# Batch 1's second transform stage rewritten from split-precision matmuls on the whole array to radix-two matmuls on its quarters

## The chip, the cores and the metric

The kernel runs on one core of one Trainium2 chip. The metric is the time of one execution on the device, in microseconds; the times given are those of three runs. The profile is one further execution, recorded by the hardware profiler. TensorE is called PE in its rows, VectorE DVE, ScalarE ACT, GpSimd POOL and SyncE SP; PEld is TensorE's weight load.

## What is computed

A long convolution over the sequence by FFT, gated by x, feeds a two-layer MLP with a leaky ReLU:

```python
h_filt = (np.maximum(pos_emb @ w1, 0.0) @ w2) * np.exp(-0.01 * pos)[:, None]
u = x * v                                   # x, v: (2, 12480, 128)
Uf = np.fft.rfft(u, n=2 * S, axis=1)
Hf = np.fft.rfft(h_filt, n=2 * S, axis=0)
y = np.fft.irfft(Uf * Hf[None], n=2 * S, axis=1)[:, :S, :]
a = (x * y).reshape(B * S, D)               # 24960 tokens of 128
h = a @ w_in                                # w_in: 128 x 2048
out = np.maximum(0.01 * h, h) @ w_out       # w_out: 2048 x 128
```

## The kernel before

The transform of a sequence is done in two stages. The first works on 98 rows of tokens and leaves 98 frequencies `k` by 64 positions `m`, real and imaginary, in DRAM (`scr1` for batch 0 and the filter, `scr1b` for batch 1). The second takes a chunk of four `k` (`KC`, so 25 chunks, `NCH`; the last holds two), transforms over the 64 positions (128 rows of real and imaginary parts), multiplies by the filter's spectrum (`hspec`), transforms back and stores to `scr2`. From there the joins (`cin`, `cp`, `cq`) and the fronts (L933 and L952: the last transform, the product with x and a transpose) make the tokens that the MLP eats.

Three stretches follow each other. Up to about 165 us batch 0 and the filter go through the first stage; its loads, and the constants, are issued by SyncE, three chunks ahead. Up to about 331 us comes batch 0's second stage (`fwd`, L136, and `back_halves`, L164). Then the MLP runs to the end over 50 column tiles of up to 512 tokens and 16 blocks of `w_in` each. Every one of these 800 slots has three matmuls of the first layer (`m1`, L1009, into `mh`, a ring of three buffers), an eviction to a high part on ScalarE (`rh`, L1013) and a low part on VectorE (`rl`, L1014), and three matmuls of the second layer (`m2`, L1050 to L1052) for the slot three earlier. Batch 1's whole transform is hidden beside the MLP of batch 0's tokens: the generator `conv1` yields it in pieces, and the loop draws so many pieces a slot as `pace` says, up to the slot `SLOTS`. The order of every engine is thus the order in which the program is written; there is no scheduler.

Batch 1's second stage is `conv1b`. For each chunk: `split` makes a high part `th` (ScalarE) and a low part `tl` (VectorE, both operands in SBUF) of the loaded `bin1`; `three` (L150) does six matmuls with `mb_h` and `mb_l` into the two `cv` banks; ScalarE brings the halves across (`usp`, L551 and L558), VectorE multiplies one product from PSUM (L553), GpSimd the other and adds (`sums`, L517 and L518); then `ph` (ScalarE) and `pl` (GpSimd, L576) split the product, and one chunk later `back` does six matmuls more, which `mixed_evac` (ScalarE, L230) takes to `ct`, one buffer, to be stored by SyncE (L221). The spectrum of a chunk is loaded by two transfers of 64 rows (L498) into `hd`. All of these are single-pass matmuls (fp32r) on 128 rows by 128 columns. Matmuls of plain fp32, as in L136, L164, L933, have two records each in the profile.

Of the kernel before, what the change touches and what calls it, by code (L numbers as in the profile page):

```python
# [8 lines left out]
F32 = mybir.dt.float32  # L9
F32R = mybir.dt.float32r  # L10
# [11 lines left out]
MC1 = 4  # L22
KC = 4
# [7 lines left out]
def tile_conv_mlp(ctx, tc, x, v, pos_emb, w1, w2, w_in, w_out, cf, cr, cg, cb, ci, cw, out):  # L31
# [20 lines left out]
    hspec = dram.tile([NCH, HB, 2, 2, 512], F32, name="hspec")  # L52
# [114 lines left out]
    def even(w):  # L167

        return (w.stop - w.start) // D % 2 == 0

    def back(dp, parts, c):

        for s in range(2):
            for j, w in halves(c):
                m = mixed if even(w) else lambda t: t
                three(dp[s][:, w], (mi_h[j][:, s], mi_l[j][:, s]), (m(parts[0][:, s, w]), m(parts[1][:, s, w])))

    def turned(pool, psum, m2, m1):
# [45 lines left out]
    def mixed_evac(dp, ct, c):

        for s in range(2):
            for _, w in halves(c):
                o, i = ct[:, w.start // D:w.stop // D, s, :], dp[s][:, w]
                if even(w):
                    nc.scalar.copy(o.rearrange("p (h k) d -> p h k d", h=2),  # L230
                                   i.rearrange("p (k d h) -> p h k d", h=2, d=D))
                else:
                    nc.scalar.copy(o, i.rearrange("p (k d) -> p k d", d=D))
            yield
# [8 lines left out]
    with tc.manual_schedule():  # L243
# [22 lines left out]
        with ExitStack() as st:  # L266
# [74 lines left out]
            nc.vector.memset(w1bd, 0.0)  # L341
            for i in range(2):
# [974 lines left out]
```

## Time and profile before

| | us |
|---|---|
| median of three runs | 1618.61 (1617.85 to 1619.16) |
| the profiled execution | 1622.39 |
| its span, first to last instruction | 1620.6 |

| engine | busy us | share of the span |
|---|---|---|
| TensorE | 1559.0 | 96% |
| VectorE | 1129.5 | 70% |
| ScalarE | 995.9 | 61% |
| GpSimd | 748.6 | 46% |

Busy shares are means over stretches with different limits. Batch 1's second stage lies between about 577 and 1013 us. A matmul's duration in the trace includes its run through the array, so that in a row of matmuls each overlaps the next: what one costs is the distance from its start to the next one's start. The same holds for queued instructions on ScalarE.

### The profile page before, as it was taken

What the parts mean: (1) busy time and instruction counts of PE and PEld (TensorE: products, weight loads), DVE (VectorE), ACT (ScalarE), POOL (GpSimd) and SP (SyncE); (2) the same over time, 40 slices, a digit from 0 to 9 for tenths busy, and PEclk for the clock granted to TensorE, in tenths of its full rate; (3) what the DMA queues carried; (4) which work ended last, traced back from release to release, by engine and by line L of the source; (5) the groups of instructions that cost most, each with busy time, mean ns of one, the idle gap of its engine ahead of it and who ended that gap; (6) DMA issues with size and microseconds to landing.
All of it is one profiled execution on the core that took longest, in us unless ns stands there. A gap on an engine that the chain in (4) does not pass through costs nothing.

```text
span 1620.6 us, 27366 instructions
## 1 busy us (share of the span) xinstructions
PE 1559.0 (96%) x9173; PEld 1323.7 (82%) x9173; DVE 1129.5 (70%) x1785; ACT 995.9 (61%) x2108; POOL 748.6 (46%) x804
## 2 busy tenths in 40 slices
PE   6798899899999999999999999999999999999999
PEld 6787555478888888888888888988888888888888
DVE  4676687765777566666677775577777777777777
ACT  2232454435655466777776777677777776777776
POOL 4563121234735257677777775453433533334310
PEclk9899999999999999999999999999999999999999
DMA  8898999966676557666656752321212212122200
GB/s 247 266 297 264 309 318 324 326 177 200 199 200 200 154 155 195 192 181 181 170 164 179 194 141 63 110 95 57 77 58 63 68 63 87 58 63 62 63 11 21
DMA packets 166358, 253.31 MB, mean 156 GB/s; under 512 B 14302, under 2 KB 119026, under 8 KB 163146
## 3 DMA queue, kind: packets, MB, share of 16 engines
q1 hardware_dynamic: 146478, 226.29, 47.2%
q10 hardware_dynamic: 19740, 25.28, 4.6%
q8 instruction: 73, 1.20, 0.3%
q14 instruction: 67, 0.55, 0.1%
HBM read 168.00 MB, written 83.43 MB: 155 GB/s over the span
## 4 chain that ended last, share of the span: by engine, by line
PE 74%; DMA 9%; DVE 6%; ACT 3%; issue 2%; SPq 1%; POOL 1%; ACTq 0%; DVEq 0%; POOLq 0%
PE mh L1009 28%; PE acc L1051 9%; PE acc L1052 9%; PE acc L1050 9%; PE yp L933 4%; PE cv L150 3%; PE cv L454 3%; DMA scr<-ct 3%; PE op L1082 2%; PE zp L952 1%; PE up L136 1%; DMA pos<-in_pos_emb_dram 1%; PE dp L164 1%; DMA scr<-o 1%; PE a L410 1%
## 5 line engine op out<-in xcount | busy, mean ns | idle before, releaser
L1014 DVE SCALAR_TENSOR_TENSOR rl<-mh,rh 128x512 fp32r<-128x512 f32 (+1 forms) x336 | 226.7, 682 | 199.1 <-ACT rh L1013 197.9
L1022 DVE TENSOR_TENSOR rl<-mh,rh 128x512 fp32r<-128x512 f32 (+2 forms) x416 | 277.2, 670 | 83.6 <-ACT rh L1021 75.0
L1017 ACT ACTIVATE mh<-mh 128x512 f32<-128x512 f32 (+2 forms) x416 | 236.3, 568 | 154.0 <-PE mh L1009 113.3
L1009 PE MATMUL mh<-zh,w_in_h 128*128 128x512 f32 (+3 forms) x800 | 316.8, 396 | 3.6 <-DVE rl L1014 2.4
L1009 PE MATMUL mh<-zl,w_in_h 128*128 128x512 f32 (+3 forms) x800 | 300.0, 375 | 0.2 <-POOL zl L966 0.2
L1009 PE MATMUL mh<-zh,w_in_l 128*128 128x512 f32 (+3 forms) x800 | 299.6, 375 | 0.0
L1051 PE MATMUL acc<-rl,w_out_h 128*128 128x512 f32 (+3 forms) x800 | 299.1, 374 | 0.1
L1050 PE MATMUL acc<-rh,w_out_h 128*128 128x512 f32 (+3 forms) x800 | 299.0, 374 | 0.0
L1052 PE MATMUL acc<-rh,w_out_l 128*128 128x512 f32 (+3 forms) x800 | 299.0, 374 | 0.0
L1013 ACT ACTIVATE rh<-mh 128x512 fp32r<-128x512 f32 (+1 forms) x336 | 198.9, 595 | 133.1 <-PE mh L1009 124.3
L966 POOL TENSOR_TENSOR zl<-zf,zh 128x390 fp32r<-128x390 f32 (+24 forms) x110 | 67.8, 630 | 426.5 <-ACT zh L965 403.8
L696 POOL TENSOR_TENSOR cp<-cq,cp 98x256 f32<-98x256 f32 x248 | 194.0, 782 | 32.6 <-DVE cp L684 15.9
L1019 DVE CAST rh<-mh 128x512 fp32r<-128x512 f32 (+2 forms) x208 | 139.3, 670 | 65.9 <-ACT mh L1017 65.5
L1009 PEld LDWEIGHTS mh<-zh,w_in_h 128*128 128x128 f32 x800 | 151.7, 190 | 29.6 <-DVE rl L1014 8.7
L1009 PEld LDWEIGHTS mh<-zh,w_in_l 128*128 128x128 f32 x800 | 151.8, 190 | 19.7
L1051 PEld LDWEIGHTS acc<-rl,w_out_h 128*128 128x128 f32 x800 | 151.2, 189 | 20.2 <-DVE rl L1022 0.4
L1050 PEld LDWEIGHTS acc<-rh,w_out_h 128*128 128x128 f32 x800 | 151.2, 189 | 19.8
L1052 PEld LDWEIGHTS acc<-rh,w_out_l 128*128 128x128 f32 x800 | 151.2, 189 | 19.7
L1009 PEld LDWEIGHTS mh<-zl,w_in_h 128*128 128x128 f32 x800 | 152.2, 190 | 15.6 <-POOL zl L966 0.6
L1021 ACT CAST rh<-mh 128x512 fp32r<-128x512 f32 (+2 forms) x208 | 118.5, 570 | 6.5
L693 POOL TENSOR_TENSOR cq<-cin 98x256 f32<-98x256 f32 x124 | 97.6, 787 | 0.3 <-DMA cin<-scr 0.3
L105 ACT COPY a1s<-a 98x384 f32<-98x384 f32 x64 | 30.7, 480 | 97.3 <-PE a L410 68.7
(170 smaller groups left out, 2529.8 us busy)
## 6 DMA issues: line engine op xcount, KB each, us to landing
cin<-scr SPq DMA_DIRECT2D x318, 98.0 KB
hd<-hspec SPq DMA_DIRECT2D x48, 512.0 KB
bin<-scr SPq DMA_DIRECT2D x23, 768.0 KB
scr<-o SPq DMA_DIRECT2D x28, 588.0 KB
scr<-ct SPq DMA_DIRECT2D x25, 512.0 KB
scr1b<-o SPq DMA_DIRECT2D x32, 392.0 KB
hspec<-hs ACTq DMA_DIRECT2D x48, 256.0 KB
xm<-in_x_dram SPq DMA_DIRECT2D x128, 96.0 KB
```

The source lines that it names most:

```text
L693: eng.tensor_tensor(out=cq[:, p], in0=ci_t[:, 0, :, 0, :], in1=ci_t[:, 0, :, 1, :], op=op)
L696: eng.tensor_tensor(out=cp[:, p, w], in0=cq[:, p], in1=cp[:, p, 1], op=op)
L1009: nc.tensor.matmul(hp, u[:, fs], m, start=(i == 0), stop=(i == 2))
L1013: nc.scalar.activation(out=split2(rh), in_=plain(hp), func=AF.Relu)
L1014: nc.vector.scalar_tensor_tensor(out=split2(rl), in0=plain(hp), scalar=0.0, in1=split2(rh), op0=ALU.max, op1=ALU.subtract)
L1017: nc.scalar.activation(out=hp, in_=hp, func=AF.Lrelu, alpha=0.01)
L1019: nc.vector.tensor_copy(split2(rh), plain(hp))
L1021: nc.scalar.copy(split2(rh), plain(hp))
L1022: nc.vector.tensor_tensor(out=split2(rl), in0=plain(hp), in1=split2(rh), op=ALU.subtract)
L1050: nc.tensor.matmul(ap, w_out_h[:, f, :], rh, start=(f == 0 and not sums(k)), stop=False)
L1051: nc.tensor.matmul(ap, w_out_h[:, f, :], rl, start=False, stop=False)
L1052: nc.tensor.matmul(ap, w_out_l[:, f, :], rh, start=False, stop=(f == NF - 1))
```

## The change

Only batch 1's second stage is done anew. The transform over 64 positions is split in even and odd positions (radix two). The load puts even rows on the upper 64 partitions and odd rows on the lower (two transfers, `scr1b[e::2]`), and `fwd2` does four fp32 matmuls of 64 by 64, one for each half of the rows and of the columns, straight from the loaded tile: no split in high and low parts. `odd` (ScalarE) copies one half's result, VectorE makes sum and difference `u`, multiplies by the imaginary part of the spectrum with a sign for each row (`q`; `sgn`), GpSimd by the real part (`p1`). Four ScalarE copies of 32 rows by 1024 bring `q` to the partner rows (`jq`), late in the chunk's pieces. One chunk later GpSimd adds (`o1`) and makes the sum and difference `pin`, and two chunks later `back2` does four 64 by 64 matmuls; two buffers `ct` are used in turn. The spectrum is stored in another order and loaded by four transfers of 32 rows, the result is stored by two transfers. Constants `mt`, `bt` and `sgn` take the place of `mb_h`, `mb_l`, `mi_h`, `mi_l`. A chunk has 23 pieces instead of 15, and the stage begins after 24 pieces of waiting instead of 12.

```diff
-    hspec = dram.tile([NCH, HB, 2, 2, 512], F32, name="hspec")
+    hspec = dram.tile([NCH, 2, HB, 2, 512], F32, name="hspec")
...
+    mt = const.tile([128, 2, HB], F32, name="mt")
+    sgn = const.tile([128, 1], F32, name="sgn")
+    bt = [const.tile([128, 128], F32, name=f"bt{j}") for j in range(2)]
...
+    def quads(dst, src):
+        for s in range(2):
+            for r in range(2):
+                nc.scalar.copy(dst[HB * s + 32 * r:HB * s + 32 * r + 32, :], src[HB * r:HB * r + 32, s, :])
...
+    def fwd2(up, t, n):
         for s in range(2):
+            for e in range(2):
+                r = slice(HB * e, HB * e + HB)
+                nc.tensor.matmul(up[e][HB * s:HB * s + HB, :n * D].rearrange("p (k d) -> p k d", d=D),
+                                 mt[r, s, :], t[r, :n, s, :], start=True, stop=True)
+    def back2(dp, pin, c):
+        for j, w in halves(c):
+            for s in range(2):
+                r = slice(HB * s, HB * s + HB)
+                for e in range(2):
+                    nc.tensor.matmul(dp[s][HB * e:HB * e + HB, w], bt[j][r, e::2], pin[r, e, w],
+                                     start=True, stop=True)
...
+            for q in range(4):
+                nc.vector.memset(sgn[32 * q:32 * q + 32], -1.0 if q % 2 else 1.0)
...
                     nc.sync.dma_start(out=mb, in_=cb)
+                    for e in range(2):
+                        nc.sync.dma_start(out=mt[HB * e:HB * e + HB].rearrange("p s (r q) -> p (s r) q", r=2),
+                                          in_=cb[e::2].rearrange("p s r q -> p (s r) q")[:, :, :32])
...
-        WAIT = 12
+        WAIT = 24
+        LAST_B = 6
...
             def fetch_h(c):
...
-                for i in range(2):
-                    nc.sync.dma_start(out=h[HB * i:HB * i + HB, :, :, :n * D], in_=hspec[c][:, :, :, :n * D])
+                for s in range(2):
+                    src = hspec[c][s].rearrange("(h q) r w -> q h r w", h=2)
+                    for i in range(2):
+                        q = h[HB * s + 32 * i:HB * s + 32 * i + 32]
...
+                    up = psc["next"]()
+                    fwd2(up, t, n)
+                    yield
...
+                    nc.scalar.copy(odd, up[1][:, :w])
+                    for i, op in enumerate((ALU.add, ALU.subtract)):
+                        nc.vector.tensor_tensor(out=u[:, i, :w], in0=up[0][:, :w], in1=odd, op=op)
+                        yield from rest(2)
+                    for i in range(2):
+                        nc.vector.scalar_tensor_tensor(out=q[:, i, :w], in0=u[:, i, :w], scalar=sgn, in1=h[:, i, 1, :w],
+                                                       op0=ALU.mult, op1=ALU.mult)
+                        nc.gpsimd.tensor_tensor(out=p1[:, i, :w], in0=u[:, i, :w], in1=h[:, i, 0, :w], op=ALU.mult)
+                        yield from rest(2)
+                    fetch_b(c + 3)
+                if 0 < c <= NCH:
...
+                    for i in range(2):
+                        nc.gpsimd.tensor_tensor(out=o1[:, i, :v], in0=o1[:, i, :v], in1=jq[:, i, :v], op=ALU.add)
                         yield
+                if c > NCH:
+                    yield from rest(LAST_B)
+                if c > 1:
+                    dp = psc["next"]()
+                    back2(dp, pin, c - 2)
+                    yield
+                if c > 1:
+                    ct = cts[c % 2]
+                    yield from back_evac(dp, ct, chunk(c - 2)[1])
+                    late = lambda c=c, ct=ct: store_back(1, c - 2, ct, nc.sync)
+                if c < NCH:
+                    jq = held[c] = pool.tile([128, 2, 512], F32, tag="q", name="jq", bufs=2)
+                    for i in range(4):
+                        o = 32 * (i ^ 1)
+                        nc.scalar.copy(jq[32 * i:32 * i + 32, :, :w], q[o:o + 32, :, :w])
                         yield
+                if 0 < c <= NCH:
+                    for i, op in enumerate((ALU.add, ALU.subtract)):
+                        nc.gpsimd.tensor_tensor(out=pin[:, i, :v], in0=o1[:, 0, :v], in1=o1[:, 1, :v], op=op)
+                        yield from rest(2)
...
-        pieces = N1 * (MC1 // 2) * 4 + WAIT + 3 + 15 * NCH - 3
+        pieces = N1 * (MC1 // 2) * 4 + WAIT + 23 * NCH + LAST_B
```

In the orders below the line numbers are those of the kernel that the order is of; in the changed one `m1` is L1012, `m2` L1053 to L1055, `rh` L1016.

TensorE at a forward visit of `conv1b`, before:

```order
L1050 MATMUL acc<-rh,w_out_h 128x512
L1051 MATMUL acc<-rl,w_out_h 128x512
L1052 MATMUL acc<-rh,w_out_l 128x512
L150 MATMUL cv<-th,mb_h 128x512
L150 MATMUL cv<-tl,mb_h 128x512
L150 MATMUL cv<-th,mb_l 128x512
L150 MATMUL cv<-th,mb_h 128x512
L150 MATMUL cv<-tl,mb_h 128x512
L150 MATMUL cv<-th,mb_l 128x512
```

and now:

```order
L1053 MATMUL acc<-rh,w_out_h 128x512
L1054 MATMUL acc<-rl,w_out_h 128x512
L1055 MATMUL acc<-rh,w_out_l 128x512
L172 MATMUL cv<-bin_7764,mt 64x512 x4
L1012 MATMUL mh<-zh,w_in_h 128x512
```

Six matmuls that fill the array have become four that fill a quarter of it each; a back visit (`L181`, `bt`) reads the same.

ScalarE about a chunk's evacuations (`ct`), before:

```order
L507 CAST th<-bin_8943 128x4x128
L1013 ACTIVATE rh<-mh 128x512
L511 CAST th<-bin_8943 128x4x128
L1013 ACTIVATE rh<-mh 128x512 x2
L230 COPY ct_9383<-cv 128x4x128
L1013 ACTIVATE rh<-mh 128x512
L230 COPY ct_9383<-cv 128x4x128
L1013 ACTIVATE rh<-mh 128x512
```

and now, where `pins` is one of the two buffers of `ct`, up to the next chunk's `odd`:

```order
L237 COPY pins<-cv 128x4x128 x2
L1016 ACTIVATE rh<-mh 128x512
L576 COPY jq<-q 32x1024 x2
L1016 ACTIVATE rh<-mh 128x512
L576 COPY jq<-q 32x1024 x2
L1016 ACTIVATE rh<-mh 128x512 x3
L546 COPY odd<-cv 128x512
```

Between two evictions `rh` stood one 512-wide instruction, or none; now two evacuations or two exchange copies stand there in a row.

SyncE in the first stage, about the loads of the constants, before:

```order
L182 DMA ph_305<-in_cf_dram 64x2x50 x2
L361 DMA mb<-in_cb_dram 128x256
L362 DMA mi<-in_ci_dram 128x256
L365 DMA mi_75<-in_ci_dram 64x128 x4
L383 DMA scr_60<-o 98x4x384 x2
```

and now:

```order
L188 DMA ph_307<-in_cf_dram 64x2x50 x2
L361 DMA mb<-in_cb_dram 128x256
L363 DMA mt<-in_cb_dram 64x4x32 x2
L365 DMA mi<-in_ci_dram 128x256
L368 DMA mi_75<-in_ci_dram 64x128 x4
L384 DMA scr_60<-o 98x4x384 x2
```

Two transfers stand ahead of those that were there.

## Rows read from the trace of the kernel before

**Rows 1.** Busy us (instructions) PE, PEld, DVE, ACT, POOL; PEclk, DMA share, GB/s.

```profile
577.00:1013.00 436.00, 430.94 (x2293) 370.70 (x2292) 290.25 (x401) 316.66 (x664) 309.81 (x301) 1.00 0.60 167
```

**Rows 2.** Waits of PE, 577 to 1013 us: total us, times, longest.

```profile
PE mh L1009 <- DVE rl L1014: 2.4, 5, 0.8
```

**Rows 3.** Waits of PEld in the same stretch.

```profile
PEld mh L1009 <- DVE rl L1014: 8.5, 16, 1.2
```

**Rows 4.** Timeline about 651 us: start, length, instruction [idle before it <-releaser].

```profile
651.05 1.08 ACT L230 COPY ct<-cv 128x512 f32<-128x512 f32 x2 [6.19 <-DMA scr<-ct]
651.69 0.48 PE L150 MATMUL cv<-th,mb_h 128*128 128x512 f32 x1 [1.84 <-ACT ct L230]
```

**Rows 5.** Timeline of PE: first of six matmuls of a back visit, and the next.

```profile
695.94 0.38 PE L150 MATMUL cv<-ph,mi_h 128*128 128x512 f32 x1
...
697.23 0.38 PE L1009 MATMUL mh<-zh,w_in_h 128*128 128x512 f32 x1
```

**Rows 6.** Timeline of PE in batch 0's second stage.

```profile
195.70 1.99 PE L164 MATMUL dp<-pin,mi 64*128 64x512 f32 x8
197.52 1.06 PE L846 MATMUL hp<-w,es 64*128 64x128 f32 x16
198.57 1.94 PE L136 MATMUL up<-bin,mb 128*64 128x512 f32 x8
200.31 1.07 PE L799 MATMUL ep<-mb,bin 128*64 128x128 f32 x16
```

**Rows 7.** Timeline of PE about a front.

```profile
627.75 0.38 PE L1052 MATMUL acc<-rh,w_out_l 128*128 128x512 f32 x1
628.06 1.97 PE L933 MATMUL yp<-cp,gt 98*64 98x128 f32 x32
629.96 0.48 PE L1009 MATMUL mh<-zh,w_in_h 128*128 128x512 f32 x1
630.28 0.38 PE L1009 MATMUL mh<-zl,w_in_h 128*128 128x512 f32 x1
```

**Rows 8.** Groups of ACT, 577 to 1013 us: xcount | busy, mean ns | idle before.

```profile
L575 ACT CAST ph<-usp 128x512 fp32r<-128x512 f32 x48 | 29.1, 628 | 0.0
...
L558 ACT COPY usp<-cv 64x512 f32<-64x512 f32 x48 | 27.8, 579 | 1.0
...
L575 ACT CAST ph<-usp 128x256 fp32r<-128x256 f32 x2 | 0.8, 412 | 0.0
```

**Rows 9.** Timeline of ACT while instructions are queued on it.

```profile
693.94 0.61 ACT L507 CAST th<-bin 128x512 fp32r<-128x512 f32 x1
694.45 0.60 ACT L1013 ACTIVATE rh<-mh 128x512 fp32r<-128x512 f32 x1
694.94 0.61 ACT L511 CAST th<-bin 128x512 fp32r<-128x512 f32 x1
```

**Rows 10.** Groups of DVE, 577 to 1013 us.

```profile
L1014 DVE SCALAR_TENSOR_TENSOR rl<-mh,rh 128x512 fp32r<-128x512 f32 x244 | 165.7, 687 | 135.3 <-ACT rh L1013 134.5
L512 DVE TENSOR_TENSOR tl<-bin,th 128x512 fp32r<-128x512 f32 x48 | 57.0, 1201 | 0.6 <-ACT th L507 0.6
L684 DVE TENSOR_TENSOR cp<-cin 98x256 f32<-98x256 f32 x37 | 32.9, 901 | 0.0
L553 DVE TENSOR_TENSOR usp<-cv,hd 128x512 f32<-128x512 f32 x48 | 32.8, 684 | 7.9 <-ACT usp L558 4.9 <-PE cv L150 1.8 <-DMA hd<-hspec 0.9
```

**Rows 11.** Line L684 on DVE, same stretch: duration ns min/median/max.

```profile
L684 DVE TENSOR_TENSOR cp<-cin x37: 407/420/2824, 577.2 to 966.9; 98x256 f32<-98x256 f32 x37
```

**Rows 12.** Groups of POOL, 577 to 1013 us.

```profile
L576 POOL TENSOR_TENSOR pl<-usp,ph 128x512 fp32r<-128x512 f32 x48 | 61.4, 1292 | 50.2 <-ACT ph L575 50.2
```

**Rows 13.** Timeline of SP's issues: start, length from first to last.

```profile
39.52 5.14 SPq L365 DMA_DIRECT2D mi<-in_ci_dram  x4
```

**Rows 14.** Window 40 to 45 us, columns of rows 1.

```profile
40.00:45.00 5.00, 5.00 (x37) 4.98 (x36) 5.00 (x10) 1.63 (x4) 2.68 (x3) 1.00 0.67 159
```

**Rows 15.** Line L498 on SP's queue, 577 to 1013 us: issue ns min/median/max.

```profile
L498 SPq DMA_DIRECT2D hd<-hspec x50: 450/578/1200, 577.4 to 974.1; - x50
```

More of the change, by code (lines that the diff above doesn't have):

```diff
@@ L220, in store_back @@
         k0, n = chunk(c)
+        if b:
+            for e in range(2):
+                eng.dma_start(out=scr2[b][k0:k0 + n].rearrange("k r (m e) d -> e (r m) k d", e=2)[e],
+                              in_=ct[HB * e:HB * e + HB, :n].rearrange("p k s d -> p k (s d)"))
+            return
         eng.dma_start(out=scr2[b][k0:k0 + n].rearrange("k r m e -> (r m) k e"),
                           in_=ct[:, :n].rearrange("p k s d -> p k (s d)"))
[L224 to L234, printed above, removed]
     def back_evac(dp, ct, n):
@@ L490, in fetch_b @@
                         "p (k s d) -> p k s d", s=2, d=D)
-                    nc.sync.dma_start(out=got[c][:, :n].rearrange("p k s d -> p k (s d)"),
-                                      in_=scr1b[:, k0:k0 + n, :])
+                    for e in range(2):
+                        nc.sync.dma_start(out=got[c][HB * e:HB * e + HB, :n].rearrange("p k s d -> p k (s d)"),
+                                          in_=scr1b[e::2, k0:k0 + n, :])
             def fetch_h(c):
-                n = chunk(c)[1]
+                w = chunk(c)[1] * D
@@ L525, in conv1b, with rest @@
                 yield
-            yield from split(0)
-            late, pins = None, {}
-            for c in range(NCH + 1):
+            late, held = None, {}
+            p1s, pins = (sc.tile([128, 2048], F32, tag="s4", name=g).rearrange("a (i h w) -> i a h w", i=2, h=2)
+                         for g in ("p1s", "pins"))
+            pin = pins[0]
+            cts = [pins[1].rearrange("p h (k d) -> p (h k) d", d=D).rearrange("p (k s) d -> p k s d", s=2),
+                   pool.tile([128, KC, 2, D], F32, tag="ct1", name="ct1", bufs=1)]
+            def rest(n):
+                for _ in range(n):
+                    yield
+            for c in range(NCH + 2):
                 if c + 1 < NCH:
@@ L560, in conv1b @@
-                    sums(us, p1, h, 1, w)
-                if c + 1 < NCH:
-                    yield from split(c + 1)
-                    fetch_b(c + 3)
-                if c:
-                    wb = chunk(c - 1)[1] * D
-                    dp = psc["next"]()
-                    back(dp, pins.pop(c - 1), c - 1)
-                    yield
-                    ct = pool.tile([128, KC, 2, D], F32, tag="ct1", name="ct1", bufs=1)
-                    yield from mixed_evac(dp, ct, c - 1)
-                    late = lambda c=c, ct=ct: store_back(1, c - 1, ct, nc.sync)
-                    yield
@@ L573, in conv1b @@
-                if c < NCH:
-                    for s in range(2):
-                        nc.scalar.copy(ph[:, s, :w], p1[:, s, :w])
-                        nc.gpsimd.tensor_tensor(out=pl[:, s, :w], in0=p1[:, s, :w], in1=ph[:, s, :w],
-                                                op=ALU.subtract)
-                        yield
+                    odd = pool.tile([128, 1024], F32, tag="pl", name="odd", bufs=1)[:, :w]
+                    u = pool.tile([128, 2, 512], F32, tag="ph", name="u", bufs=1)
```

72 lines of the change are left out of this document (17 added, 55 removed).

## The prediction

> **What bounds the kernel now.** I first read the busy times of the stretch that holds the changed work, batch 1's second stage [rows 1]: TensorE is busy for 430.94 of 436 us at a granted clock of 1.00, the 2.4 GHz level. VectorE (290), ScalarE (317) and GpSimd (310) each have about 30% to spare, so only three things count: the time that the stage's matmuls occupy on TensorE, the waits that the other engines put into TensorE's row, and what the change adds elsewhere. Then TensorE's waits [rows 2, 3]: as the matmul row shows them, 2.4 us for `rl` (VectorE's half of an eviction) in 5 waits, and seen from the weight loads, which run ahead, 8.5 us in 16. The remaining large one is one wait of about 2 us: ScalarE stood 6.19 us before `ct`, whose only buffer was still being stored, and TensorE's next matmul there came at 651.69 [rows 4]. So this stretch is TensorE's, with some 5 to 7 us of stalls.
>
> **TensorE: two visits a chunk.** Before, a visit is six single-pass matmuls on the whole array: 697.23 - 695.94 = 1.29 us [rows 5], or 0.216 each. There are two visits in each of 25 chunks; the last chunk is half as wide, so they amount to 49 full ones, 63.2 us. After, a visit is four two-pass matmuls of 64 rows by 64 columns, one to each quarter of the array. The trace has quarters in no row, but it has both halves: four matmuls on half of the columns each (L136) take 200.31 - 198.57 = 1.74 us, four on half of the rows each (L164) 197.52 - 195.70 = 1.82 us [rows 6], two at a time in both, as their eight records would take 8 x 0.43 one by one. Four at a time should take half, 0.87 to 0.91, and I take 0.89. Around it comes a switch of the array's division, which the front's matmul (L933) shows [rows 7]: it starts 0.31 after the last full one instead of 0.216 (+0.09); its 16 pair slots of 128 columns, at 1.74/16 = 0.109 each, should take 1.74 and take 629.96 - 628.06 = 1.90 (+0.16); the first full matmul behind it takes 0.32 instead of 0.216 (+0.10). That is 0.35 a visit. So after: 49 x 0.89 + 50 x 0.35 = 61.1 us, against 63.2: **-2.1 us**. Most of what the quarters save goes into the switches. The bounds: with 0.86 and a switch of 0.30, -6; if three more starts each add 0.04 to a visit (half of 1.82 - 1.74, an estimate), so 0.11, +3.4.
>
> The Trainium skill says in "TensorEngine Tiling (Array Packing)", Key Properties, that changing the tiling mode drains the engine while tiles run independently; the first half agrees with the 0.31 above, and no run here shows four tiles. It speaks against the change: without that drain the sum of this part would be -20.
>
> **ScalarE: the same total, in longer pieces.** Before, ten 512-wide instructions a chunk of 0.58 to 0.63 us [rows 8], 6.0 us. After, three of these (`odd`, two evacuations) and four exchange copies of 1024 elements on 32 rows. The cast of 512 takes 0.628 and that of 256 0.412 [rows 8], so 1024 take 0.628 + 2 x 0.216 = 1.06; together 3 x 0.59 + 4 x 1.06 = 6.0 us. What counts is the bunching. Queued instructions start 0.50 to 0.51 apart [rows 9] though each takes 0.6, so a queued exchange copy costs about 0.95, an evacuation or `rh` about 0.49.
>
> The order of the new kernel puts, behind a back visit: two evacuations, `rh`, two copies, `rh`, two copies, `rh`. With time zero at the visit's end, the expansion's group i starts on TensorE at 1.295 i (six matmuls), and its `rh` can start 0.85 later (third matmul at 0.43, 0.38 long, a hand-over of 0.04). ScalarE: evacuations 0.20 to 1.15; rh0 at 1.15; copies to 3.55; rh1 at 3.55 (due at 2.14); copies to 5.94; rh2 at 5.94 (due at 3.44), 2.5 us late. `rl` follows: 0.60 + 0.69 + 0.08 of hand-overs, so the buffer of group 2 is free at 7.31. The ring has three buffers; group 5 wants it at 5 x 1.295 = 6.48, which alone would be a stall of 0.8 a chunk, 21 us in all. But between groups 4 and 5 now stands the next forward visit, 1.24 us, so group 5 is due at 7.72: 0.4 us to spare. Group 4 needs group 1's buffer at 3.55 + 1.37 = 4.92 and is due at 5.18, 0.26 to spare. So the bunch fits, by 0.3 to 0.4 us, where a `rh` that starts on time has 3 x 1.295 - 0.85 - 1.37 = 1.66.
>
> **What eats that margin.** VectorE is sometimes late: `tl`, with two operands in SBUF, takes 1.2 us on the mean against 0.68 for L553 of the same size with an operand in PSUM; the joins' `cp` (L684) takes 0.90 on the mean, 0.42 in the median and up to 2.8 [rows 10, 11]; both run while GpSimd, busy 71% [rows 1], works in SBUF. The 16 waits of [rows 3] among 244 groups are such lateness beyond 1.66, one in 15; beyond 0.35 I estimate one in 8. With two thin groups in each of 25 bunches that gives 6 hits of some 0.6 us, **+3.5 us**, bounds 0 and 15 (every bunch hit).
>
> The Trainium skill ("SBUF — State Buffer", Who interferes with whom) says that a VectorE instruction with two SBUF inputs is shut out while GpSimd reads SBUF. The 1.2 against 0.68 agree; by it the new `q` (two SBUF operands, issued beside GpSimd's product) is no cheaper than `tl`.
>
> **VectorE, GpSimd, SyncE.** VectorE has four 512-wide instructions a chunk before (two `tl`, two products from PSUM) and four after (two sums from PSUM at 0.68, two `q` with both operands in SBUF, 1.2 as `tl`). GpSimd has six before and six after, at 1.29 each [rows 12]. No change there. `ct` has two buffers in turn now, so the wait of [rows 4] goes: **-2.0 us** (next late there is the bunch above). SyncE issues four more transfers a chunk, for the same bytes: 100 at some 0.58 us [rows 15], 58 of 436 us, on a queue that nothing in [rows 2] waits for; behind them stand the joins' loads: 0, and up to 2 where a load comes late. The early loads are different: two transfers for `mt` (32-element pieces) join the four of `mi2` on SyncE's queue, which took 5.14 us to issue, 1.3 each [rows 13], and in that stretch the DMA engines were busy only 0.67 [rows 14]; behind them stand the stores and the x and v loads that the first stage waits for. Two more: 2.6 us of issue, a quarter to a third of it lost transfer time: **+0.8 us**, bounds 0 and 2.6. `sgn`'s four memsets and the four small copies into `bt` lie before waits for first loads: 0. The spectrum is stored in pieces twice as long, same bytes: 0 (at best -1).
>
> **The sum.** -2.1 + 3.5 - 2.0 + 0.8 = +0.2 us on a profiled execution of 1622.4 us (span 1620.6). That one is 3.8 us above the median of the runs, 1618.6, so I add the change to the median: **1618.8 us**, no change. A measurement of this kernel tells about 0.2%, 3.2 us, from no change.
>
> **Rivals.**
> 1. *Faster: VectorE's lateness no longer meets TensorE.* `q` is issued right behind the forward visit, one block apart, where 1.66 us and a visit lie ahead, while `tl` came two at once. Then the stalls of [rows 2] and [rows 3] (about 5 us by the matmuls' starts, between 2.4 and 8.5) shrink to 1, and the visits come at the low bound: -4 - 4 - 2 + 0.8 = -9, half of it -5: 1612 us (1609 to 1615). For it: equal totals on all engines. Against: the thin margins. Chance 0.32.
> 2. *Slower: the bunch does not fit.* It decides from 0.3 us on: if the copies take 1.06 each queued rather than 0.95, rh2 comes 0.44 later and each bunch stalls, and a late `cp` adds to it. At 0.5 us for 25 bunches, +12.5 in place of +3.5: 1628 us (1622 to 1634). For it: margin 0.26 against 1.66. Against: fronts and transposes put more TensorE time between. Chance 0.20.
> 3. *Four tiles run short of four-fold.* With a stagger of 0.11 to 0.16 us a visit, +5.5 to +8 against the sum: 1626 us. Chance 0.05. The Trainium skill's "TensorE: Matmul & The Clock Gate", Part 3, gives 3.07-fold for four tiles on rows, by which the quarters would take 3.5/3.07 = 1.13 instead of 0.89.
> 4. *The quarters run only two at a time*, as every row here does: 1.74 a visit instead of 0.89, 49 x 0.85 = +42: 1661 us. Against: the four write separate halves of two banks, as the halves do. Chance 0.04.
>
> My forecast has 0.39. The range 1609 to 1630 takes in rival 1 and most of 2 and 3 and leaves out rival 4 and the tails. Faster by over 0.2%: 0.34 (rival 1, and the low end of the forecast); within: 0.37; slower: 0.29 (rivals 2 to 4 all but whole).
>
> **What will show it.** A visit (first quarter matmul to the next full one) of 0.95 to 1.05, eight records within 0.45 us of each other in two slots, says that quarters run four wide; 1.8 or more says rival 4. The exchange copy should read 1.06 us alone. TensorE's waits for `rl` in the stretch should stay between 6 and 12 us seen from the weight loads: below 4 is rival 1, above 18 is rival 2. The wait for `ct` should be gone. The 40 to 48 us stretch should show six slow issues. I am wrong where TensorE waits for something not named here, such as GpSimd's `pin` before a back visit.

## The result, and the profile after

The changed kernel takes 1641.2 us in the median of five runs (1637.46 to 1645.58); the kernel before took 1618.61 beside it (1617.39 to 1619.50). The ratio is 1.0146, interval 1.0123 to 1.0168: **slower by 23 us**, above the whole range of 1609 to 1630. The profiled execution has a span of 1639.4 us, against 1620.6.

The loss lies in batch 1's second stage. The first row is TensorE's waits in matmuls from 577 to 1033 us (the stage now ends 20 us later), the second the same waits seen from its weight loads: total us, times, longest. The third is the stretch of [rows 1] in the same columns.

```profile
PE mh L1012 <- DVE rl L1017: 22.8, 19, 4.0
PEld mh L1012 <- DVE rl L1017: 54.4, 50, 4.5
577.00:1013.00 436.00, 412.58 (x2280) 309.97 (x2279) 306.70 (x385) 309.50 (x554) 297.12 (x289) 0.98 0.63 163
```

Against [rows 2, 3] the waits for `rl` went from 2.4 to 22.8 us, and from 8.5 to 54.4 by the weight loads. VectorE is busy for 307 us instead of 290, with the same number of its own instructions in each chunk. Its groups, and GpSimd's, from 577 to 1033 us (count, busy us, mean ns of one, idle before):

```profile
L551 DVE SCALAR_TENSOR_TENSOR q<-u,sgn,hd 128x512 f32<-128x512 f32 x48 | 85.7, 1793 | 0.0
L687 DVE TENSOR_TENSOR cp<-cin 98x256 f32<-98x256 f32 x36 | 35.8, 1009 | 0.0
L548 DVE TENSOR_TENSOR u<-cv,odd 128x512 f32<-128x512 f32 x48 | 32.2, 680 | 6.3 <-ACT odd L546 6.2
...
L560 POOL TENSOR_TENSOR p1s<-p1s,jq 128x512 f32<-128x512 f32 x48 | 69.6, 1467 | 0.0
L553 POOL TENSOR_TENSOR p1s<-u,hd 128x512 f32<-128x512 f32 x48 | 64.4, 1351 | 57.4 <-issue 41.6 <-DVE u L548 15.6
L580 POOL TENSOR_TENSOR pins<-p1s 128x512 f32<-128x512 f32 x48 | 61.1, 1289 | 2.4 <-PE cv L181 2.1
```

`u`, with one operand in PSUM, takes 0.68 us, as L553 did in [rows 10]. `q` has both operands in SBUF and takes 1.79 us on the mean, where the prediction gave it `tl`'s 1.2; two each chunk make 85.7 us where `tl` had 57.0. A typical bad place, in the timelines of GpSimd, VectorE and TensorE (start, length, instruction; the row at 673.04 is the second of the two `q` of the row above it):

```profile
667.46 2.52 POOL L553 TENSOR_TENSOR p1s<-u,hd 128x512 f32<-128x512 f32 x2
669.93 0.74 POOL L696 TENSOR_TENSOR cq<-cin 98x256 f32<-98x256 f32 x1
670.62 1.27 POOL L560 TENSOR_TENSOR p1s<-p1s,jq 128x512 f32<-128x512 f32 x1
671.85 0.73 POOL L699 TENSOR_TENSOR cp<-cq,cp 98x256 f32<-98x256 f32 x1
672.52 1.72 POOL L560 TENSOR_TENSOR p1s<-p1s,jq 128x512 f32<-128x512 f32 x1
...
667.57 7.22 DVE L551 SCALAR_TENSOR_TENSOR q<-u,sgn,hd 128x512 f32<-128x512 f32 x2
673.04 1.74 DVE L551 SCALAR_TENSOR_TENSOR q<-u,sgn,hd 128x512 f32<-128x512 f32 x1
674.71 1.87 DVE L1017 SCALAR_TENSOR_TENSOR rl<-mh,rh 128x512 fp32r<-128x512 f32 x3
...
671.02 0.38 PE L1055 MATMUL acc<-rh,w_out_l 128*128 128x512 f32 x1
675.44 0.80 PE L1012 MATMUL mh<-zh,w_in_h 128*128 128x512 f32 x1 [4.05 <-DVE rl L1017]
```

Two `q` take 7.22 us, the first of them 5.55, while GpSimd runs six instructions from 667.46 to 674.24, each of which begins as the one before it ends (669.98 and 669.93, 671.89 and 671.85). The first `q` ends at 673.12, 0.55 us behind the end of the fifth of these (672.57), and the sixth takes 1.72 us instead of 1.27: so this `q` stood behind five instructions and got in at the end of the fifth, though GpSimd did not pause there. The second got in behind the sixth. No `rl` can pass the two `q` on VectorE's queue; three are late, and TensorE stands for 4.05 us. Then it runs at half clock for a while, as the windows behind that wait show (columns of [rows 1]):

```profile
674.00:677.00 3.00, 1.56 (x4) 1.29 (x5) 2.58 (x4) 1.04 (x1) 3.00 (x4) 0.50 0.33 110
677.00:680.30 3.30, 3.30 (x10) 2.58 (x8) 0.69 (x1) 2.68 (x3) 0.84 (x1) 0.50 0.00 0
680.30:684.00 3.70, 3.70 (x20) 3.26 (x19) 0.69 (x1) 2.69 (x4) 0.00 (x0) 0.98 0.05 13
```

The granted clock is 0.50, the 1.2 GHz level, up to 680.3, and ten matmuls of the MLP start 0.427 apart instead of 0.216. There are four such places; 27 starts at that distance cost 27 x 0.21 = 5.7 us, where the kernel before has two.

From the first matmul of the MLP's first layer to the last, the stretch is 1294.5 us instead of 1271.6, so 22.9 more: +20.4 of waits for `rl` (22.8 - 2.4), +5.3 of half clock, -2.0 for `ct`, -3.7 for the visits (49 x 1.02 + 50 x 0.19 against 63.2, with what the rows below show of a visit); 2.9 us are not assigned.

What was predicted of the visit and of the copies stands in these rows of TensorE and ScalarE:

```profile
668.50 0.38 PE L1055 MATMUL acc<-rh,w_out_l 128*128 128x512 f32 x1
668.81 1.09 PE L181 MATMUL cv<-pins,bt 64*64 64x512 f32 x8
669.83 0.48 PE L1012 MATMUL mh<-zh,w_in_h 128*128 128x512 f32 x1
670.15 0.38 PE L1012 MATMUL mh<-zl,w_in_h 128*128 128x512 f32 x1
...
656.91 2.11 ACT L576 COPY jq<-q 32x1024 f32<-32x1024 f32 x2
659.04 0.60 ACT L1016 ACTIVATE rh<-mh 128x512 fp32r<-128x512 f32 x1
659.66 1.04 ACT L576 COPY jq<-q 32x1024 f32<-32x1024 f32 x1
```

The eight records of the quarters start in two slots (0, 7, 14 and 20 ns; then 480 ns and on) and the visit takes 669.83 - 668.81 = 1.02 us: four run at a time. A copy takes 1.04, and two queued ones 2.11, so 1.06 from one to the next: nothing of a copy is hidden by the next one, as it was for the instructions of [rows 9].

### The profile page after: what moved, and what is told of

Its sections match the earlier page's. It is cut to its first block, busy times and chain, and to the rows that moved or that the text cites. A ratio compares the mean times of both kernels' runs of the same rounds, so it can differ in the third digit from the quotient of the medians.

```text
span 1639.4 us, 27658 instructions
## 1 busy us (share of the span) xinstructions
PE 1560.4 (95%) x9275; PEld 1278.0 (78%) x9275; DVE 1152.3 (70%) x1786; ACT 1006.3 (61%) x2036; POOL 745.3 (45%) x804
## 4 chain that ended last, share of the span: by engine, by line
PE 70%; DVE 11%; DMA 10%; ACT 4%; issue 3%; SPq 1%; POOL 1%; ACTq 0%; DVEq 0%; POOLq 0%
PE mh L1012 28%; PE acc L1054 9%; PE acc L1055 9%; PE acc L1053 9%; PE yp L936 4%; PE cv L456 3%; DMA scr<-o 3%; DVE q L551 2%; ACT jq L576 2%; DMA ft<-in_cf_dram 2%; PE op L1085 2%; DVE rl L1017 1%; PE zp L955 1%; PE up L135 1%; DMA scr<-ct 1%
## 5 line engine op out<-in xcount | busy, mean ns | idle before, releaser
L1012 PE MATMUL mh<-zh,w_in_h 128*128 128x512 f32 (+3 forms) x800 | 324.1, 405 | 24.1 <-DVE rl L1017 22.8
L1012 PE MATMUL mh<-zl,w_in_h 128*128 128x512 f32 (+3 forms) x800 | 301.1, 376 | 0.0
L1012 PE MATMUL mh<-zh,w_in_l 128*128 128x512 f32 (+3 forms) x800 | 300.9, 376 | 0.0
L1053 PE MATMUL acc<-rh,w_out_h 128*128 128x512 f32 (+3 forms) x800 | 300.3, 375 | 0.0
L1055 PE MATMUL acc<-rh,w_out_l 128*128 128x512 f32 (+3 forms) x800 | 300.1, 375 | 0.0
L1016 ACT ACTIVATE rh<-mh 128x512 fp32r<-128x512 f32 (+1 forms) x336 | 195.5, 594 | 136.3 <-PE mh L1012 127.8
L1012 PEld LDWEIGHTS mh<-zh,w_in_h 128*128 128x128 f32 x800 | 152.5, 191 | 91.4 <-DVE rl L1017 54.6
L1012 PEld LDWEIGHTS mh<-zh,w_in_l 128*128 128x128 f32 x800 | 152.5, 191 | 20.0
L1055 PEld LDWEIGHTS acc<-rh,w_out_l 128*128 128x128 f32 x800 | 151.9, 190 | 20.0
L1053 PEld LDWEIGHTS acc<-rh,w_out_h 128*128 128x128 f32 x800 | 151.8, 190 | 20.1
L1012 PEld LDWEIGHTS mh<-zl,w_in_h 128*128 128x128 f32 x800 | 153.0, 191 | 13.9 <-DVE zl L1001 0.2
L576 ACT COPY jq<-q 32x1024 f32<-32x1024 f32 (+1 forms) x100 | 102.7, 1027 | 9.3 <-DVE q L551 7.4
```

The costliest lines, as they stand in the source:

```text
L576: nc.scalar.copy(jq[32 * i:32 * i + 32, :, :w], q[o:o + 32, :, :w])
L1012: nc.tensor.matmul(hp, u[:, fs], m, start=(i == 0), stop=(i == 2))
L1016: nc.scalar.activation(out=split2(rh), in_=plain(hp), func=AF.Relu)
L1053: nc.tensor.matmul(ap, w_out_h[:, f, :], rh, start=(f == 0 and not sums(k)), stop=False)
L1055: nc.tensor.matmul(ap, w_out_l[:, f, :], rh, start=False, stop=(f == NF - 1))
```

## The experiments

Theory A: VectorE's instructions with two operands in SBUF, `q` above all and the joins' `cp` beside it, are shut out for as long as GpSimd's instructions follow one another without a gap. Rivals: B, the bunch of ScalarE's copies makes `rh`, and so `rl`, late; C, the joins' `cp` alone. Each table row below is one run; "before" took 1617.9, 1617.5 and 1618.0 us in the three groups of runs. Waits are those of TensorE's matmuls and of its weight loads for `rl` from 577 to 1033 us, in the one profiled execution of each kernel. That one lies within 4 us of the kernel's median, but for e9, where it is the longest of ten (1619.3 us).

| kernel | median us | ratio to before (interval) | waits, matmuls | weight loads |
|---|---|---|---|---|
| before | | | 2.4 | 8.5 |
| changed | 1641.2 | 1.0146 (1.0123 to 1.0168) | 22.8 | 54.4 |
| e1, `q` from PSUM | 1622.0 | 1.0026 (1.0012 to 1.0039) | 7.7 | 29.1 |
| e2, half copies | 1628.4 | 1.0070 (1.0048 to 1.0092) | 12.6 | 40.9 |
| e3, gaps | 1623.3 | 1.0031 (1.0016 to 1.0045) | 10.4 | 42.5 |
| e4, sums in PSUM | 1644.5 | 1.0166 (1.0137 to 1.0195) | 5.2 | 24.8 |
| e5, spectrum alone | 1617.7 | 1.0006 (0.9990 to 1.0022) | 2.3 | 8.4 |
| e6, before, no dependent neighbours | 1634.1 | 1.0096 (1.0081 to 1.0111) | 12.2 | 18.8 |
| e7, copies apart | 1633.1 | 1.0108 (1.0075 to 1.0140) | 20.3 | 41.2 |
| e8, gaps, copies apart | 1618.0 | 1.0007 (0.9991 to 1.0022) | 6.5 | 30.5 |
| e9, e4 with a later back visit, copies apart | 1612.5 | 0.9979 (0.9963 to 0.9995) | 5.6 | 19.1 |
| e10, e9 with the joins moved | 1608.6 | 0.9939 (0.9925 to 0.9954) | 2.1 | 17.6 |
| e11, e4 with copies apart | 1640.0 | 1.0153 (1.0120 to 1.0186) | 1.2 | 13.6 |
| e12, changed with the joins moved | 1627.7 | 1.0062 (1.0040 to 1.0084) | 15.2 | 49.5 |

**Where `q` reads from.**

```diff
-  nc.vector.scalar_tensor_tensor(out=q[:, i, :w], in0=u[:, i, :w], scalar=sgn, in1=h[:, i, 1, :w],
+  nc.vector.scalar_tensor_tensor(out=q[:, i, :w], in0=u[:, i, :w], scalar=sgn, in1=up[i][:, :w],
```

> The changed kernel, with one operand of VectorE's product q taken from PSUM (the forward visit's result) instead of the spectrum's tile in SBUF; so q leaves out the spectrum's imaginary part and keeps its size, place and one SBUF operand. Theory A (q has two operands in SBUF and is shut out while GpSimd's instructions, none of which waits for its neighbour, follow each other without a gap; rl stands behind it): q falls from 1.79 us on the mean to 0.75, the weight loads' waits for rl from 54 us to under 12, and the time from 1641 to 1612 to 1620 us. Theory B (ScalarE's exchange copies of 1.04 us bunch and make rh late): q shortens, but the time stays within 6 us of 1641. Theory C (the joins' cp on VectorE, shut out in the same way, does it): q shortens, cp stays at about 1.0 us, the time falls by less than half, to 1630 or above.

```profile
L551 DVE SCALAR_TENSOR_TENSOR q<-u,sgn,cv 128x512 f32<-128x512 f32 x48 | 34.9, 736 | 0.0
...
L181 PE MATMUL cv<-pins,bt 64*64 64x512 f32 (+3 forms) x208 | 31.8, 590 | 0.7 <-ACT ct L237 0.7
```

`q` takes 0.74 us, always, and 19 of the 23 us are gone: 1622.0 us. That is 2 us above what A expected, and the weight loads' waits, 29.1 us where under 12 were expected, say that `q` is not all of it. The second row, of TensorE from 577 to 1045 us, says where some of it went: the back visits' quarters hold TensorE for 31.8 us, where the changed kernel has 26.9 in the same row, probably because `q` now reads the two banks that they write.

**The length of the copies.** Only one half of `q` is exchanged, and taken for both.

```diff
-  nc.scalar.copy(jq[32 * i:32 * i + 32, :, :w], q[o:o + 32, :, :w])
+  nc.scalar.copy(jq[32 * i:32 * i + 32, 0, :w], q[o:o + 32, 0, :w])
```

> The changed kernel, with the four exchange copies of a chunk half as long (512 elements instead of 1024; the second half of the exchange is left out and GpSimd adds the first half twice). It takes 4 x 0.43 = 1.7 us from every chunk's bunch on ScalarE. Theory A (q shut out by GpSimd): q and the waits for rl stay, 1635 to 1641 us. Theory B (the bunch): the margin of the third rh grows from 0.4 to over 1.6 us, the waits for rl fall below 15 us and the time to 1622 or less.

1628.4 us lies between the two expectations. The bunch counts, with 13 us, but `q` stays at 1.64 us on the mean and 40.9 us of waits remain. Neither theory does alone.

**Gaps on GpSimd.**

```diff
+  def gap(t):
+      nc.gpsimd.tensor_tensor(out=dot, in0=t, in1=t, op=ALU.add)      # dot: 128 x 1
   nc.gpsimd.tensor_tensor(out=p1[:, i, :w], in0=u[:, i, :w], in1=h[:, i, 0, :w], op=ALU.mult)
+  gap(p1[:, i, w - 1:w])
   nc.gpsimd.tensor_tensor(out=o1[:, i, :v], in0=o1[:, i, :v], in1=jq[:, i, :v], op=ALU.add)
+  gap(o1[:, i, v - 1:v])
```

> The changed kernel, with a GpSimd addition of one element behind each of the chunk's two products p1 and two sums o1, which reads what that instruction has just written; results are the same. GpSimd then does four small instructions more a chunk (some 0.2 us each, 20 us in all), and has a gap of about 0.08 us before each, as it had before the change between its dependent product and sum. Theory A in its narrow form (VectorE gets in at a gap of GpSimd): q falls from 1.79 us to 1.2 on the mean with none above 2.5 us, and the time to 1615 to 1625 us. Theory A in its wide form (what counts is how long GpSimd is busy in SBUF, gaps or not): q stays at 1.8 or more, the time at 1641 or above. Theory B: 1641.

A hundred instructions more for GpSimd, with nothing taken away, and the kernel is 18 us faster, 1623.3 us. The timelines of GpSimd and VectorE at one such place:

```profile
784.81 0.73 POOL L703 TENSOR_TENSOR cq<-cin 98x256 f32<-98x256 f32 x1
785.50 1.27 POOL L558 TENSOR_TENSOR p1s<-u,hd 128x512 f32<-128x512 f32 x1
786.85 0.52 POOL L525 TENSOR_TENSOR dot<-p1s 128x1 f32<-128x1 f32 x1
...
784.86 2.46 DVE L556 SCALAR_TENSOR_TENSOR q<-u,sgn,hd 128x512 f32<-128x512 f32 x1
787.25 0.68 DVE L1024 SCALAR_TENSOR_TENSOR rl<-mh,rh 128x512 fp32r<-128x512 f32 x1
```

`q` is queued at 784.86 and still stands behind `cq` and `p1`, which join without a gap (785.54 and 785.50). Behind `p1`, from 786.77 to 786.85, GpSimd waits for its own result, 0.08 us, and there `q` gets in: the `dot` then takes 0.52 instead of 0.19, and `q` ends at 787.32. The longest `q` of the stretch is 2.55 us, where the changed kernel has 5.58; the mean is 1.33, both a little above what A's narrow form expected.

So theory A holds in part. A `q` needs some 0.55 us from where it gets in (673.12 - 672.57 above), so its end tells at which boundary between two GpSimd instructions that was. In the changed kernel the 50 `q` met 4 boundaries with a pause and got in at each; of 69 without one they got in at 34 and were passed over at 35, up to four times in a row. In e3 they got in at all 34 with a pause; without one, at 5 of 20. In no run here was a `q`, a `tl` or a `cp` passed over at a pause. What decides at a boundary without a pause, no run shows.

**Everything from PSUM.** `u` is made in place in the two banks, and VectorE makes both products from there; GpSimd has four instructions a chunk left.

```diff
-  nc.vector.tensor_tensor(out=u[:, i, :w], in0=up[0][:, :w], in1=odd, op=op)
+  nc.vector.tensor_tensor(out=up[1][:, :w], in0=up[0][:, :w], in1=odd, op=ALU.subtract)
+  nc.vector.tensor_tensor(out=up[0][:, :w], in0=up[0][:, :w], in1=odd, op=ALU.add)
...
-  nc.gpsimd.tensor_tensor(out=p1[:, i, :w], in0=u[:, i, :w], in1=h[:, i, 0, :w], op=ALU.mult)
+  nc.vector.tensor_tensor(out=p1[:, i, :w], in0=up[i][:, :w], in1=h[:, i, 0, :w], op=ALU.mult)
```

> The changed kernel, with sum and difference u written in place into the PSUM banks of the forward visit, and both products (q and p1) made by VectorE from there, so that no VectorE instruction of the chunk has two SBUF operands and GpSimd has four instructions a chunk instead of six; results are the same. VectorE has six instructions of 0.68 to 0.75 us a chunk. Theory A: the waits for rl fall below 12 us, 1611 to 1618 us, below both kernels (visits 3 us shorter, the stretch up to the MLP's start 4 us earlier, as in the changed kernel's trace). Theory B: 1635 or above. If VectorE's six instructions in ten pieces are too dense: 1620 to 1630.

A's 1611 to 1618 us is missed. 1644.5 us lies where B expected it, but not for B's reason: `q` takes 0.74 us, and the weight loads' waits for `rl` shrink from 54.4 to 24.8 us with the bunch as it was. TensorE's rows, the last one that of the changed kernel:

```profile
PE cv L181 <- DVE p1s L556: 6.0, 9, 1.6
...
L181 PE MATMUL cv<-pins,bt 64*64 64x512 f32 (+3 forms) x208 | 45.2, 594 | 9.0 <-DVE p1s L556 6.0 <-ACT ct L237 2.1 <-ACT pins L237 0.7
...
L181 PE MATMUL cv<-pins,bt 64*64 64x512 f32 (+3 forms) x208 | 26.9, 590 | 0.0
```

The last product reads the two `cv` banks late in the chunk's pieces, and the back visit that follows wants the same two: its quarters hold TensorE for 45.2 us instead of 26.9. Of these 18.3 us the waits of the matmuls show 6.0 for the product; much of the rest counts as busy, between records of the visit. Counted from the start of the last full matmul ahead of a back visit to the first one behind it, the 25 back visits take 60.0 us instead of 35.1, so 25 us more. Two further kernels tell whether that is the loss. In both, the copies are set apart, with a piece of other work behind each (e7's edit, below); e9 moves the back visit behind the first two of them as well.

```diff
+  yield from exchange(0)
+  yield                       # one piece of the MLP
+  yield from exchange(1)
   dp = psc["next"]()
   back2(dp, pin, c - 2)
   yield
   yield from back_evac(dp, ct, chunk(c - 2)[1])
+  yield from exchange(2)
+  yield from added(0)         # first half of pin
+  yield from exchange(3)
+  yield from added(1)
```

> As e4_sums_in_psum (sums made in place in PSUM, VectorE takes both products from there), but the back visit comes three pieces later, behind two of the exchange copies, and the copies stand apart. In e4's trace the back visits' matmuls held TensorE for 45.2 us instead of 26.9, waiting for the product that still read the two banks they write. If that wait was e4's loss (18 us, and some 4 us of half clock behind it): 1612 to 1622 us, the back visits at 27 to 29 us. If VectorE's six instructions a chunk were too much for it: 1632 to 1645 us, with the waits at rl instead.

> e4_sums_in_psum (1644.5 us) with the exchange copies set apart, and the back visit where it was, so that it and e9_psum_late_visit (1612.5 us) differ in the place of the back visit and of two copies. If the back visit's wait for its two banks is e4's loss: still 1632 to 1644 us, back visits 42 to 47 us of TensorE. If e9's gain came from the copies: 1612 to 1620 us.

```profile
L181 PE MATMUL cv<-pins,bt 64*64 64x512 f32 (+3 forms) x208 | 30.3, 607 | 0.0
...
L181 PE MATMUL cv<-pins,bt 64*64 64x512 f32 (+3 forms) x208 | 44.8, 591 | 12.4 <-DVE p1s L556 9.5 <-ACT ct L237 2.1 <-ACT pins L237 0.7
```

The first is e9: 30.3 us, a little above the 27 to 29 expected, and a time of 1612.5. e11, with the visit where it was, has 44.8 us in the same row and takes 1640.0, though its matmuls' waits for `rl` (1.2 us) are below those of the kernel before. By the starts of the full matmuls around them, the back visits take 35.8 us in e9 and 63.0 in e11: these 27 us are the whole difference of the two times. So e4's loss was the wait for the banks.

**Copies apart.**

```diff
   for i in range(4):
       nc.scalar.copy(jq[32 * i:32 * i + 32, :, :w], q[o:o + 32, :, :w])
       yield
+      if i % 2 == 0:
+          nc.gpsimd.tensor_tensor(out=pin[:, i // 2, :v], ...)
+      yield
-  for i, op in enumerate((ALU.add, ALU.subtract)):
-      nc.gpsimd.tensor_tensor(out=pin[:, i, :v], ...)
-      yield from rest(2)
```

> The changed kernel, with ScalarE's four exchange copies set apart: behind the back visit one copy, then a piece of other work, then the next, so that one rh stands between any two copies instead of pairs of copies; the same instructions otherwise. In the changed kernel TensorE waits for rl 54.6 us by the weight loads, and e2_half_copies, with copies of half the length, waited 40.9 and took 1628.4 us. Theory A (q, shut out by GpSimd's instructions that follow one another without a gap, makes rl late; the bunch of copies only takes the margin away): the long q of 4 to 5.6 us stay, and with them waits of 2 to 4 us; time 1628 to 1636 us, waits by the weight loads 35 to 48 us. Theory B (the bunch alone decides): 1614 to 1620 us, waits under 15 us.

> The two cures together: a one-element dependent addition on GpSimd behind each product and each sum (as in e3_gaps, 1623.3 us, 42.5 us of waits for rl by the weight loads) and the exchange copies set apart. If both causes count (A for the length of q, B for the margin): 1612 to 1619 us, below the kernel before, since the stretches ahead of the MLP are some 4 us shorter in the changed kernel's trace; waits by the weight loads under 20 us. If the bunch does not count at all: 1621 to 1625 us, as e3_gaps.

e7 takes 1633.1 us, with `q` at 1.83 us and waits of up to 4.1 us as before: A. Set apart, the copies bring 8 us; gaps alone bring 18 (e3), both together 23 (e8, 1618.0 us). e8 is level with the kernel before, not below it as expected, and 30.5 us of weight-load waits are left where under 20 were expected. So the bunch is a real but smaller part, and `q` the larger one.

**The joins' `cp`.**

```diff
-  eng = nc.vector if t == 0 or 8 <= t < NT else nc.gpsimd
+  eng = nc.vector if t == 0 else nc.gpsimd
```

> The changed kernel with the joins' first sums (cp, 36 instructions, 35.8 us of VectorE) on GpSimd and nothing else changed: VectorE has 36 us less to do, GpSimd 28 us more, and its instructions stand closer still. Theory A: q is shut out as before or longer (mean 1.8 to 2.3 us), time 1636 to 1648 us. Theory C (the joins' cp on VectorE, up to 2.9 us each, is what makes rl late): 1622 to 1632 us.

> e9_psum_late_visit (1612.5 us), with the joins' first sums (cp, 36 instructions of 0.90 us on VectorE there, with two operands in SBUF) on GpSimd, which stands idle for 207 of 436 us there. Theory A, taken further: cp is then the last instruction of VectorE that GpSimd can shut out, so the remaining waits for rl by the weight loads fall from 19 to under 10 us, time 1607 to 1611.5 us. If those waits are the bunch's alone: 1611 to 1615 us.

e12 takes 1627.7 us: the time is where C expected it, and A was wrong to expect no gain. But C alone does not hold either, with 49.5 us of weight-load waits left. `q` is hardly shorter (1.66 us on the mean, the longest 5.89), but the matmuls' waits fall from 22.8 to 15.2 us with `cp` off VectorE's queue. `cp` is the same kind of instruction, up to 2.92 us long in the changed kernel, and the second victim. e10, where nothing on VectorE's queue in this stage has both operands in SBUF any more, is the fastest kernel here, 1608.6 us, 0.6% below the kernel before. Its waits and the stretch of [rows 1]:

```profile
PE mh L1029 <- DVE rl L1034: 2.1, 2, 1.8
PEld mh L1029 <- DVE rl L1034: 17.6, 23, 2.0
577.00:1013.00 436.00, 433.89 (x2446) 333.09 (x2445) 268.32 (x422) 330.76 (x596) 248.11 (x283) 1.00 0.65 167
```

The weight loads' waits stayed at 17.6 where under 10 were expected, and the matmuls hardly feel them (2.1 us). In the trace, 12.4 us of these, in 16 of 23 waits, ended with an `rl` that had itself waited for its `rh` on ScalarE, and in 13 of the 16 an exchange copy ran right ahead of that `rh`; the other 5.2 us stood in VectorE's own queue.

**The kernel before, the other way round.** GpSimd's two products and two sums of a chunk, where each sum stood right behind its product, are issued as products first, then sums. The first product and its sum also come two pieces later than they did, so that all four stand in one row.

```diff
-  if s:
-      sums(us, p1, h, 0, w)       # product 0, sum 0
...
-  sums(us, p1, h, 1, w)           # product 1, sum 1
+  for s in range(2):
+      nc.gpsimd.tensor_tensor(out=us[:, s, :w], in0=us[:, s, :w], in1=h[:, 1, s, :w], op=ALU.mult)
+  for s in range(2):
+      nc.gpsimd.tensor_tensor(out=p1[:, s, :w], in0=p1[:, s, :w], in1=us[:, s, :w], op=ALU.add)
```

> The kernel before, with GpSimd's four instructions a chunk on the spectrum in another order: two products, then two sums, behind one another, where each product was followed at once by the sum that needs it; the same results. In the kernel before, such dependent neighbours leave 0.08 us between them, and VectorE's tl (two operands in SBUF) begins or ends there. Theory A (a stretch of GpSimd's instructions without a gap shuts out VectorE's instruction with two operands in SBUF): tl's mean rises from 1.20 to 1.4 to 1.9 us, waits for rl by the weight loads rise from 8.5 to 15 to 30 us, time 1621 to 1632 us. If the gaps play no part and q is slow for what it is (a scalar per partition, another operation): tl stays at 1.20 us, time 1616 to 1620 us.

The same instructions on every engine, in another order on one that is busy for 71% of the stretch, and the kernel before becomes 16 us slower: 1634.1 us, 2 us more than A expected at most. That the first product comes later makes TensorE wait for nothing: its waits for `pl`, which is made from the sums, are 0.2 us as before. VectorE's groups, then GpSimd and VectorE at 700 us:

```profile
L512 DVE TENSOR_TENSOR tl<-bin,th 128x512 fp32r<-128x512 f32 x48 | 63.5, 1335 | 0.6 <-ACT th L507 0.6
L685 DVE TENSOR_TENSOR cp<-cin 98x256 f32<-98x256 f32 x36 | 36.0, 1014 | 0.0
...
699.03 2.52 POOL L559 TENSOR_TENSOR usp<-usp,hd 128x512 f32<-128x512 f32 x2
701.50 2.52 POOL L561 TENSOR_TENSOR usp<-usp 128x512 f32<-128x512 f32 x2
703.98 0.91 POOL L694 TENSOR_TENSOR cq<-cin 98x256 f32<-98x256 f32 x1
...
700.07 5.10 DVE L685 TENSOR_TENSOR cp<-cin 98x256 f32<-98x256 f32 x2
```

The means rise little (1.20 to 1.34, below the 1.4 expected; 0.90 to 1.01), but the longest `tl` goes from 2.36 to 5.96 us and the longest `cp` from 2.82 to 4.29. Five waits of 1.9 to 2.7 us come of it, and 24 starts at half clock behind four of them (24 x 0.21 = 5.0 us).

**The spectrum's store.**

```diff
-  hspec = dram.tile([NCH, HB, 2, 2, 512], F32, name="hspec")
+  hspec = dram.tile([NCH, 2, HB, 2, 512], F32, name="hspec")
```

> The kernel before, with one part of the change: the spectrum is stored in DRAM in pieces of 4 KB, the real and the imaginary half apart, and read back by four transfers of 64 rows a chunk. In the changed kernel the MLP's first matmul comes 4.1 us earlier (337.8 against 341.9 us) with the first stages otherwise as before. If the longer pieces of the spectrum's store are what saves this: the first MLP matmul at 337 to 339 us and a time of 1613 to 1616 us. If it is the lighter preparation of the matrices (no splits for them): 341 to 342.5 us and 1617 to 1620 us.

1617.7 us, ratio 1.0006 (0.9990 to 1.0022): no difference. Its first MLP matmul comes at 338.1 us, as the first answer expected, but in e6, whose stages ahead of the MLP are those of the kernel before, it comes at 338.7 against 341.9 there. So the 4 us by which the changed kernel's MLP begins earlier lie within what one execution differs from the next, and the question rested on nothing.

## Why the prediction was wrong

- **TensorE's visits, -2.1 us: right.** The quarters take 1.02, the entry 0.31 and the first full matmul behind 0.32, where 0.216 is the rule for each: 1.02 + 0.09 + 0.10, some 1.21 us where 1.24 was predicted, which makes the sum -3.7. Rival 4 is out, and so is rival 3: with four at a time the eight records took two slots, not more.
- **The wait for `ct`, -2.0: right.** No row of the changed kernel's matmul waits names it.
- **ScalarE's copies: the length right, the queue wrong.** 1.04 us against 1.06. But the step "a queued exchange copy costs about 0.95" was taken from instructions of 512 elements on 128 partitions, whose starts lie closer than they are long; here queued copies start 1.06 apart. `rh2` is late by four times 0.11 more than worked out, and the margin of 0.26 to 0.4 us is gone. That is the point from which rival 2 was to decide, and the bunch did cost something: e2, e7, and e8 beside e3 put it at 5 to 13 us.
- **VectorE and GpSimd, "No change there": the step that failed most.** The prediction gave `q` the mean of `tl`, 1.2 us, since both have two operands in SBUF, and let the totals stand. The duration belongs not to the instruction but to its neighbour on the other engine. In the kernel before, each product on GpSimd is followed by the sum that needs it, so that GpSimd pauses for 0.08 us (L517 from 693.84 to 695.13, L518 from 695.21), and `tl` waits for one or two instructions at most (it was passed over at 2 boundaries and got in at 38). The change issues GpSimd's work as pairs that don't need each other (two `p1`, two `o1`, two `pin`), with the joins' between them, and `q` beside them. e3 restores the pause and takes 18 us back; e6 takes it away from the kernel before and costs that one 16 us; e1 frees `q` of the second operand and takes 19 back. The three go the same way from both sides, so that the second operand and GpSimd's order cost these 16 to 19 us is shown, not argued.
- **The margin, +3.5, bounds 0 and 15: mis-sized.** It measured 20.4 us of waits more, and 5.3 of half clock behind them, for which the sum had no term. The hits are not "some 0.6 us" but up to 4.
- **The sign for rival 2 came, but it could not tell the cause.** Above 18 us from the weight loads was to mean that the bunch does not fit; it is 54.4, and e7, with the copies apart, still has 41.2. Rival 2's price (0.5 us for 25 bunches, 12.5) is about what the bunch costs, 5 to 13 us; what it left out is `q`.
- **Rival 1's sum** takes -4 for the visits at their low bound, which is -6 in the part on TensorE; its full effect would be -11 us, not -9.
- **Early loads, +0.8, and the spectrum, 0.** The window of [rows 14] reads 0.71 for the DMA share after the change. The two new issues take 1.25 us, half of what was expected, and the four old ones 3.32 instead of 5.14; the store behind them starts at 45.23 us instead of 44.77. e5 gives 0 for the spectrum. The start of the MLP differs by more than 3 us between executions, so 0.8 can't be told.

The Trainium skill says in "SBUF — State Buffer", Who interferes with whom, that such a VectorE instruction contends with a GpSimd instruction that reads SBUF, for the shared read interface, under an exclusive lock. Every row here agrees: 0.74 us with one operand in PSUM, 1.79 with two in SBUF. By that rule alone one expects to wait for one instruction of GpSimd, 1.3 us. The 5.55 us behind five of them, and the 35 of 69 boundaries at which a `q` was passed over, show that the wait can run over several; the pauses, at which none was passed over, end it.

What stays open: how e12's gain divides between fewer instructions on VectorE's queue and the `cp` that were shut out, what lets a `q` in at some boundaries without a pause and not at others, and how much of e10's 17.6 us of weight-load waits the copies make. Its trace names them for the larger part, but no run took them out of e10.

## What to carry to other kernels

Price a VectorE instruction with two operands in SBUF not by its mean in another order, but take as a bound the longest row of GpSimd instructions without a dependence that may stand beside it; read one operand from PSUM, or let GpSimd's neighbours depend on each other. Whoever keeps an operand in PSUM to that end must ask which matmul wants the bank next (25 us in e4), and free it first. A wait of some us in TensorE's row can cost more than its length, since half clock followed the four longest ones of the changed kernel (2.0 to 4.05 us).

## What was not expected of the hardware

- GpSimd's instructions that need nothing of each other leave no gap, and a VectorE instruction with two operands in SBUF was shut out over five of them, 5.55 us for 0.74 us of work. It got in at about half of such boundaries; a pause of 0.08 us let it in each time. Adding a hundred instructions of 0.31 us made the kernel 18 us faster.
- Four fp32 matmuls on the four quarters of the array run at a time: eight records in two slots, 1.02 us.
- Queued ScalarE copies of 1024 elements on 32 partitions start 1.06 us apart at a length of 1.04; those of 512 elements on 128 partitions start 0.50 apart at 0.60.
